# Block-sparse attention and a gated FFN in one kernel: a new start, recalibrated plan durations, and new load and work orders

## The chip, the cores and the metric

One core of one Trainium2 chip (trn2). The metric is the device time of one execution in microseconds (us). Kernels are compared in rounds on the same chip. Some executions come out slower, most of them with a lower mean TensorE clock (of the kernel before, for example, 260.20 us at 0.986 against 254.04 at 1.000); runs are marked fast or slow. In the views, PE is TensorE and PEld its weight loads, ACT is ScalarE, DVE is VectorE, POOL is GpSimd, and SP is SyncE, which here only issues transfers.

## The reference

Attention for 4 batches, 8 heads, 768 positions, head size 64, with a block mask (neighbours, first and last blocks, three random blocks per row), then a gated FFN on the 3072 x 512 result:

```python
scores = np.matmul(q, k.transpose(0, 1, 3, 2)) / np.sqrt(D)
scores = np.where(mask, scores, -1e9)          # mask: 24 x 24 blocks of 32
attn = exp(scores - max); attn = attn / (sum(attn) + 1e-9)
x = np.matmul(attn, v)                         # then (tokens, 512)
h = (x @ w1) * (x @ w2) @ w3                   # d_ff 1024
out = h @ w_out                                # float32
```

## The kernel before

The kernel describes its work as tasks with durations and dependences. A small list scheduler (`Plan.run`) orders them before anything is built; the chip then executes that order, engine by engine. A wrong duration cannot make a wrong result, but it can put a waiting instruction in front of others on an engine that works in order.

The work of one score tile: 4 matmuls (TensorE, here PE) into PSUM, one exp (ScalarE, ACT), half of a multiplication by the mask (VectorE, DVE), 8 value matmuls. There are 144 tiles, 36 per batch: 4 head pairs x 3 groups of 256 queries x 3 parts of the keys. The FFN of 512 tokens is 64 + 32 matmuls of 512 columns, six times; w3 and w_out are first multiplied together (64 more). q and k must be transposed: the first `trb` = 8 pairs (b, pr) on PE, the rest by a DMA transpose that SP issues:

```python
# (parts that the argument touches; cuts marked ...)
PRM = dict(bias=0.4, ..., btc=0.5, near=0.12, soon=0.06, kprio=2.0, ..., trb=8, units="tttt", nat=4, big=10)
...
    # if PE has nothing to do in the plan, it runs a "spare" matmul on zeros
    if pe > free["PE"] + 0.12 and rest > free["PE"] - 0.1:
        w = self.spare(mode)                     # planned at 0.11 us each
...
    elif t.kind == "xbar":                       # a DMA transpose
        busy = [row for a, z, row in lanes if a < t.start + 1.25 <= z]
        more = 4.0 * max(busy) / 4096 if busy else 0.0
        t.end = t.start + 1.25 + more            # time on SP
        t.seen = t.end + 2.6 + more              # landing
...
    nc.scalar.preload_act_table_set("natural_log_exp_and_others")
...
    for nm, dst, src, at in (("qn", q32, qv, 4.0), ("kn", k32, kv, 5.0)):   # first q and k, both from SP
        ld = add(f"first {nm}", {SP: 0.43}, lambda t, ...: nc.sync.dma_start(out=dst, in_=src[0][:, 0:2]), ...)
        LD[nm, 0, 0] = add(f"cast {nm}", both(0.81, 0.5), ...)              # one cast on ACT or DVE
...
            else:                                # pairs beyond trb
                m = add(f"re {b}{pr}{x}", {DVE: 0.37}, ... T("qs", ...) <- T("qn", ...).rearrange("p h c d -> p c h d"))
                t = add(f"xb {b}{pr}{x}", {SP: 1.25}, ... nc.sync.dma_start(out=qkt, in_=qs, transpose=True), kind="xbar")
```

All other loads of q, k, v and the weights are issued by GpSimd, in the order of a table `LOADS` ("a01" is q and k of pair (0,1), "v00" v of pair (0,0), "p20" all three of pair (2,0), "30" a part of w3, "10" and "20" parts of w1 and w2, "o0" of w_out).

The softmax here doesn't subtract the row's maximum and nothing guards it: scores larger than these inputs give would overflow.

## Time and profile before

| | before |
|---|---|
| median of the runs with the prediction | 254.35 us (254.33 to 254.66) |
| span of the profiled execution | 252.7 us |
| PE / ACT / DVE busy | 95% / 74% / 69% |
| first score, tile 12, tile 48, PE's end | 9.88, 30.30, 76.51, 248.83 us |

"Tile n" is the time at which the weight load of score tile n starts. These four times turn a busy timeline into progress; the prediction shows the lines of the profile and how to read them.

### The profile page before, as it was taken

The numbers are of one execution on the slowest core, as the hardware profiler recorded it, in microseconds if no ns is written. First come the engines' busy times: TensorE is split into PE (matmuls) and PEld (weight loads), VectorE is DVE, ScalarE is ACT, GpSimd is POOL, SyncE is SP. The second block draws the span as 40 slices with busy tenths as digits, with TensorE's granted clock in tenths as the row PEclk, the third lists the DMA queues.
The fourth block names the chain that finished last, engine by engine and source line by source line (L and its number), as shares of the span: only waits on it lengthen the run. The fifth ranks groups of instructions, "written<-read, shape, count | busy, mean of one in ns | idle before, by whom it ended". The sixth has DMA issues, their size and how long they took to land.

```text
span 252.7 us, 6330 instructions
## 1 busy us (share of the span) xinstructions
PE 240.6 (95%) x2647; PEld 130.5 (52%) x2689; DVE 174.9 (69%) x305; ACT 186.4 (74%) x231; POOL 44.9 (18%) x73
## 2 busy tenths in 40 slices
PE   7989999997999999999999999999999999999993
PEld 5554655664555455455455445555555554444441
DVE  5696698899699897988856776878777754312320
ACT  3685788897889898889888888788988862323321
POOL 8635455444421360000000000000000000000000
PEclk9999999999999999999999999999999999999998
DMA  7999999999997899994142020231201223022013
GB/s 174 171 205 207 208 210 194 164 199 167 177 173 99 104 144 194 184 242 86 34 110 101 4 42 3 61 108 44 42 4 21 65 89 79 0 83 83 4 42 125
DMA packets 45793, 28.08 MB, mean 111 GB/s; under 512 B 27332, under 2 KB 40644, under 8 KB 45764
## 3 DMA queue, kind: packets, MB, share of 16 engines
q0 software_dynamic: 15872, 14.29, 38.2%
q1 hardware_dynamic: 29892, 13.38, 25.4%
q8 instruction: 21, 0.34, 0.6%
q14 instruction: 8, 0.07, 0.1%
HBM read 29.36 MB, written 6.29 MB: 141 GB/s over the span
## 4 chain that ended last, share of the span: by engine, by line
PE 86%; DVE 4%; DMA 4%; ACT 3%; issue 2%; SPq 0%
PE f L622 33%; PE f L642 17%; PE s L528 14%; PE o L551 14%; PE f L603 5%; DMA x<-xn 4%; PE o L397 2%; DVE e L538 2%; ACT e L534 2%; PE f L474 1%; PE f L591 1%; DVE xn L561 1%; ACT qkt L293 0%; DVE w3t L293 0%; SPq L574 0%
## 5 line engine op out<-in xcount | busy, mean ns | idle before, releaser
L534 ACT ACTIVATE e<-s 128x1024 bf16<-128x1024 f32 x144 | 139.6, 1025 | 13.5 <-PE s L528 12.8
L622 PE MATMUL f<-x,w 128*128 128x512 bf16 x359 | 90.4, 379 | 2.8 <-issue 1.0
L538 DVE TENSOR_TENSOR e<-e,mask 128x2048 bf16<-128x2048 bf16 x72 | 87.4, 1218 | 7.4 <-ACT e L534 7.1
L551 PEld LDWEIGHTS <-e 128*128 128x128 bf16 x1152 | 44.1, 97 | 22.9 <-DVE xn L561 6.5
L633 DVE TENSOR_TENSOR big<-f,a 128x512 bf16<-128x512 f32 x48 | 33.1, 689 | 32.0 <-PE f L622 24.9
L551 PE MATMUL o<-v,e 128*128 128x65 bf16 x1152 | 50.6, 194 | 0.8 <-DVE xn L561 0.4
L622 PEld LDWEIGHTS <-w 128*128 128x128 bf16 x384 | 32.4, 98 | 35.3 <-issue 6.7
L642 PE MATMUL f<-wf,big 128*128 128x512 bf16 x183 | 46.2, 380 | 0.9 <-issue 0.6
L630 ACT CAST a<-f 128x512 bf16<-128x512 f32 x48 | 28.2, 588 | 24.6 <-PE f L622 24.6
L528 PE MATMUL s<-qkt 64*128 64x256 bf16 x576 | 45.2, 272 | 0.7 <-ACT e L534 0.7
L528 PEld LDWEIGHTS <-qkt 64*128 64x128 bf16 x576 | 22.2, 94 | 27.5 <-issue 24.1
L642 PEld LDWEIGHTS <-big 128*128 128x128 bf16 x192 | 16.1, 98 | 17.3 <-issue 3.2
L293 ACT COPY ob<-f 128x512 f32<-128x512 f32 x20 | 11.7, 587 | 14.1 <-PE f L642 14.1
L561 DVE TENSOR_TENSOR xn<-o,rec 128x256 bf16<-128x256 f32 x48 | 20.4, 424 | 1.7
L559 DVE RECIPROCAL rec<-o 128x4 f32<-128x4 f32 x48 | 8.6, 179 | 17.3 <-PE o L551 17.3
L603 PE MATMUL f<-wo,w3t 128*128 128x512 bf16 x56 | 15.8, 380 | 0.6 <-issue 0.3
L331 POOL DMA_DIRECT2D qn<-in_q_dram x15 | 10.9, 727 | 18.9 <-DVE qs L483 5.3
L331 POOL DMA_DIRECT2D kn<-in_k_dram x15 | 10.8, 719 | 14.1 <-DVE qs L483 6.2
L331 POOL DMA_DIRECT2D vn<-in_v_dram x16 | 11.4, 716 | 8.2 <-DVE v L496 5.8
L397 PE MATMUL o<-zero 128*128 128x256 bf16 (+1 forms) x45 | 7.8, 331 | 1.5 <-DVE zero L394 1.5
L293 DVE COPY qkt<-f 128x768 bf16<-128x768 bf16 x13 | 7.1, 552 | 2.0 <-PE f L474 1.9
L603 PEld LDWEIGHTS <-w3t 128*128 128x128 bf16 x64 | 4.9, 98 | 5.0 <-issue 0.6
(54 smaller groups left out, 87.1 us busy)
## 6 DMA issues: line engine op xcount, KB each, us to landing
out_dram<-ob SPq DMA_DIRECT2D x24, 256.0 KB, 2.0
vn<-in_v_dram POOLq DMA_DIRECT2D x16, 192.0 KB, 7.8
qn<-in_q_dram POOLq DMA_DIRECT2D x15, 192.0 KB, 8.1
kn<-in_k_dram POOLq DMA_DIRECT2D x15, 192.0 KB, 8.1
big<-in_moe_w_dram POOLq DMA_DIRECT2D x8, 256.0 KB, 8.9
w<-in_moe_w_dram POOLq DMA_DIRECT2D x8, 256.0 KB, 9.7
wo<-in_moe_w_out_dram POOLq DMA_DIRECT2D x2, 512.0 KB, 9.4
q<-in_q_dram SPq DMA_DIRECT2D x1, 384.0 KB, 3.2
```

What stands on the lines that cost most here:

```text
L293: (nc.scalar.copy if t.eng == ACT else nc.vector.tensor_copy)(out, in_)
L331: t = add(name, {POOL: 0.73}, lambda t: nc.gpsimd.dma_start(out=out_of(), in_=src), deps=deps, writes=writes, kind="load", prio=seq[0])
L528: nc.tensor.matmul(s[:, h, k2 * QT:(k2 + 1) * QT], lhsT=z[64 * h:64 * h + 64, 1, kc * 128:(kc + 1) * 128], rhs=z[64 * h:64 * h + 64, 0, t3 ...
L534: exps.append(add(f"E {m} {j}", {ACT: 0.97}, lambda t, sk=sk, ek=ek, j=j: nc.scalar.activation(T(*ek)[:, j], T(*sk), AF.Exp, scale=1.0 / 8 ...
L538: tm = add(f"K {m}", {DVE: 1.23}, lambda t, ek=ek, t3=t3, kp=kp: nc.vector.tensor_tensor(T(*ek), T(*ek), mask[:, t3, kp:kp + 2, :].unsquee ...
L551: nc.tensor.matmul(o[:, qt, h, :], lhsT=e[:, j, h, lo:lo + 128], rhs=w[:, h, kc, :], start=kc == 0 and qt == 0 and h == 0, stop=kc == C - ...
L561: tx = add(f"xn {rk}", {DVE: 0.42}, lambda t, rk=rk, ok=ok, xk=xk, pr=pr: nc.vector.tensor_tensor(T(*xk)[:, :, 128 * pr:128 * pr + 128].re ...
L603: nc.tensor.matmul(T(*key), lhsT=T("w3t", i)[:, j, :], rhs=wo_sb[:, j, :], start=j == 0, stop=j == NF - 1)
L622: nc.tensor.matmul(T(*key), lhsT=w[:, c, f * 128:(f + 1) * 128], rhs=T(*xk)[:, c, :], start=c == 0, stop=c == 3)
L630: ta = add(f"a {i}{f}", {ACT: 0.58}, lambda t, ak=ak, key=ends["w1"][0]: nc.scalar.copy(T(*ak), T(*key)), deps=[ends["w1"][1]], reads=[end ...
L633: nc.vector.tensor_tensor(T(*hk)[:, 512 * (f % 2):512 * (f % 2) + 512], T(*key), T(*ak), op=ALU.mult),
L642: nc.tensor.matmul(T(*key), lhsT=T(*hk[f // 2])[:, 512 * (f % 2) + n * 128:512 * (f % 2) + (n + 1) * 128], rhs=wf_sb[:, f, :], start=f == ...
```

## The change

The intent: q and k of the first pair sooner (k issued from ACT's queue ahead of the table load, casts in halves on two engines, written in a layout that needs half as many transposes); plan durations from measurements; loads in a new order (q and k of batch 0 first); and scheduling parameters that were searched anew, `trb=6` among them, so that pairs (1,2) and (1,3) move to the DMA transpose.

```diff
-SEEN = {"PE": 0.22, "ACT": 0.10, "DVE": 0.10, "POOL": 0.12, "SP": 0.05}
-SWITCH = 0.095
-LOADS = ("a01 v00 v01 o0 o1 30 a02 v02 31 32 a03 v03 33 34 35 36 37 "
-         "10 20 11 21 12 22 13 23 p10 p11 p12 p13 "
-         "p20 p21 p22 p23 p30 p31 p32 p33")
+SEEN = {"PE": 0.195, "ACT": 0.15, "DVE": 0.135, "POOL": 0.12, "SP": 0.05}
+SAME = {"PE": 0.0, "ACT": 0.13, "DVE": 0.118, "POOL": 0.05, "SP": 0.0}
+SWITCH = 0.1
+WARM = 4.9
+LOADS = ("a01 v00 a02 o1 a03 30 v01 v02 31 o0 32 34 33 v03 37 10 35 36 20 21 11 22 13 23 p13 12 "
+         "p10 p12 p11 p21 p20 p22 p23 p32 p30 p31 p33")
-PRM = dict(bias=0.4, ..., trb=8, units="tttt", ...)
+PRM = dict(bias=0.182, ..., trb=6, units='ttQt', ...)
@@ spares: planned at twice 0.11 us before WARM, so fewer of them
-                if pe > free["PE"] + 0.12 and rest > free["PE"] - 0.1:
+                if pe > free["PE"] + 0.12 * (2 if free["PE"] < WARM else 1) and rest > free["PE"] - 0.1:
+                    cost = w.costs["PE"] * (2 if free["PE"] < WARM else 1)
@@ start
-    nc.scalar.preload_act_table_set("natural_log_exp_and_others")
+    for nm, dst, src, eng, at in (("qn", q32, qv, SP, 3.9), ("kn", k32, kv, ACT, 4.3)):
+        ld = add(f"first {nm}", {eng: 0.46}, ... (nc.sync if t.eng == SP else nc.scalar).dma_start(...))
+        for hf in range(2):
+            LD[nm, 0, 0, hf] = add(f"cast {nm} {hf}", both(0.35, 0.22), ...)   # into [128, C, 2, D]
+    add("table", {ACT: 1.29}, lambda t: nc.scalar.preload_act_table_set(...), prio=-1.5)
-    t_zero = add("zero", {DVE: 0.2}, ...)
+    t_zero = add("zero", {POOL: 0.2}, ...)
@@ first pair: 6 full transposes each for q and k, copied out by halves (cut)
@@ all durations of the plan (cut), for example
-            exps.append(add(f"E {m} {j}", {ACT: 0.97}, ...
+            exps.append(add(f"E {m} {j}", {ACT: 0.915}, ...
```

## The prediction

> **What bounds the kernel now.** I read the page first: the busy shares, the slices, the chain that ended last.
>
> ```profile
> PE 240.6 (95%) x2647; PEld 130.5 (52%) x2689; DVE 174.9 (69%) x305; ACT 186.4 (74%) x231; POOL 44.9 (18%) x73
> ...
> PE   7989999997999999999999999999999999999993
> ...
> PEclk9999999999999999999999999999999999999998
> DMA  7999999999997899994142020231201223022013
> ...
> PE 86%; DVE 4%; DMA 4%; ACT 3%; issue 2%; SPq 0%
> ```
>
> PE (TensorE) is busy nearly everywhere and makes 86% of the chain, at full granted clock. But busy is not useful: in the first slices PE runs "spare" matmuls on zeros, and the DMA engines are full until about 100 us. So I split the run by the windows view (columns: stretch, its length, then busy us of PE, weight loads, DVE, ACT, POOL, clock, DMA share, GB/s).
>
> ```profile
> 6.80:69.00 62.20, 58.24 (x841) 35.33 (x850) 49.69 (x91) 49.95 (x61) 30.12 (x47) 1.00 1.28 192
> 69.00:206.90 137.90, 135.34 (x1579) 72.19 (x1602) 109.41 (x181) 119.71 (x144) 8.58 (x12) 1.00 0.51 89
> 206.90:248.90 42.00, 41.71 (x204) 19.10 (x206) 11.79 (x19) 14.10 (x25) 0.00 (x0) 1.00 0.16 54
> ```
>
> Then the timeline of the start, and the chain in order of time.
>
> ```profile
> 0.74 1.28 ACT L324 ACT_TABLE_LOAD   x1 [0.74 <-PEq L677]
> 1.25 0.46 SPq L347 DMA_DIRECT2D k<-in_k_dram  x1
> 1.47 5.41 PE L397 MATMUL o<-zero 128*128 128x256 bf16 x31 [1.47 <-DVE zero L394]
> 3.92 0.83 ACT L293 CAST qn<-q 128x768 bf16<-128x768 f32 x1 [1.91 <-DMA q<-in_q_dram]
> 5.15 0.16 DVE L418 CAST rand_f<-rand_sb 24x3 f32<-24x3 int32 x1 [1.27 <-DMA rand_sb<-in_sampled_blocks_dram]
> 6.03 0.54 DVE L293 CAST kn<-k 128x768 bf16<-128x768 f32 x1
> 6.81 0.53 PE L474 MATMUL f<-ident,qn 128*64 128x128 bf16 x12
> 8.23 0.53 PE L474 MATMUL f<-ident,kn 128*64 128x128 bf16 x12 [0.47 <-ACT qkt L293]
> 9.89 0.61 PE L528 MATMUL s<-qkt 64*128 64x256 bf16 x8
> ```
>
> ```profile
> 52.34 9.25 DMA x<-xn
> ...
> 67.43 1.30 PE f L622 x6
> 68.72 0.54 PE s L528 x8
> 69.27 0.97 PE f L622 x4
> 70.23 0.24 PE o L551 x8
> 70.48 0.86 PE f L622 x4
> ```
>
> q is cast by 4.75, but PE stays in its 31 spares until 6.81; k is cast only at 6.03, behind DVE work that waited for the random blocks. The first score is at 9.89, the first exp at 10.32. From about 69 us PE is simply full.
>
> **A ledger of PE work.** From the chain: a 512-column matmul takes 0.2165 us (32 of L642 in 6.91); four take 0.86, or 0.97 next to a score run, so a switch between 64-row scores and 128-row work costs 0.11 each way; eight score matmuls take 0.54 with one switch, so 0.0535 each; a value matmul 0.0304 (16 in 0.49); a transpose 0.0292 in pairs of half tiles (12 weight loads in 0.36), 0.0535 for w3; a mask matmul 0.107. The instruction order gives the counts: 576 score, 1152 value, 640 of 512 columns, 192 q/k and 64 w3 transposes, 20 mask, 76 score runs. Sum 215.6, plus 76 x 0.22 = 16.7: **232.3 us**. Check: by the ledger 171.6 us lie between score tile 48 and PE's end; the trace has that tile at 76.51 and the end at 248.86, 172.35. So after tile 48 only 0.75 us are wasted. Real work begins at 6.81, so 248.86 - 6.81 - 232.3 = 9.75 us of starvation lie almost wholly before tile 48. By tile: 0 at 9.88, 12 at 30.30 (ledger 17.8 by then), 42 at 68.78, 48 at 76.51. Thus **the end is tile 12's time, plus the ledger from there, plus the starvation still to come**; after PE, the last copy and store take 3.84 to the span's end, and the measured time is 254.35 - 252.7 = 1.65 over the span.
>
> **What the Trainium skill says.** (1) "TensorE: Matmul & The Clock Gate", Part 1: the array runs at half clock until some 3.4 us of sustained activity. The trace agrees: spares' weight loads are 0.213 us apart until 5.29 us, then 0.107; that is why 31 spares planned at 0.11 ran till 6.50 and held the transposes back. (2) "DMA: Bandwidth & Descriptors", Issuing engines are not separate DMA queues: transfers issued from several engines share the 16 DMA engines, and another issuer saves only sequencer time. The trace has k issued 0.51 us after q on one queue, landing 3.7 against 3.2 us after issue; so I grant the move of k some 0.5 us, not parallel bandwidth. (3) "ScalarE: Activation LUTs", What ACT_TABLE_LOAD costs: about 1283 ns; the trace has 1283 ns, from 0.74 to 2.02. Behind the k issue it ends near 2.5, before q lands at 3.9: no cost. (4) "TensorEngine Tiling (Array Packing)", Tiling Modes: changing the mode drains TensorE; the trace agrees with 0.11 us a switch.
>
> **The change part by part.**
> Start. k is issued near 0.74 and should land by 4.5. The casts are halved over ACT and DVE: about 0.3 instead of 0.83 (q, ACT) or 0.54 (k, DVE). Only 14 spares stand before the transposes; at 0.213 they end near 4.4. Casting into the [c,2,d] layout makes 12 full transposes of 24 half ones. The DVE order still has rand_f before k's half cast, and rand landed about 5.0; its issue moves up 0.5. So: q transposed 4.5 to 5.2, k cast by 5.2, transposed by 5.8, both copied by 6.6 (DVE's three random-block steps, 3 x 0.23, come between), first score near **6.7 instead of 9.88**. ACT now copies G (0.6 + 0.36) before the first exp, so that is near 7.4, not 10.3: 2.9 us won.
> First tiles. The loads now take q and k of all batch-0 pairs first (at the 0.2 MB/us of before, the third q/k pair lands near 10.5 and the fourth near 15.5), so scores no longer wait on w3 and w_out. Until tile 12 ACT paces it: 11 exps at 0.92 start to start (1.94 for two) and six copies of 0.59 make 13.7 us after 7.4: tile 12 at **21.1 instead of 30.3**. Of these 9.2 us most is only order: PE's ledger at tile 12 is 12.1, not 17.8, as w3 work has moved behind. Net 9.2 - 5.7 = 3.5 us.
> PE work. Two pairs (1,2) and (1,3) go from PE transposes to the DMA transpose: 48 fewer at 0.0292, 1.4 us. The first pair is neutral. Score runs rise from 76 to 78: +0.44. Ledger of after: **231.3**, so 1.0 us won. DVE exchanges PSUM copies of 0.56 for SBUF ones of 0.35; off the path.
> Rest of the schedule. New order, load order and a third batch by pair groups change no work, only starvation. Before, 248.86 - 30.30 - (232.3 - 17.8) = 4.1 us come after tile 12. The largest visible one is the first FFN matmul waiting for x: 9.25 us of transfer among full DMA engines. By its order, PE of after reaches the last value matmul of the second token group near 40.5 and the first FFN matmul after 12 us more work, which just covers such a transfer. I guess 2.3 us left: 1.8 won.
> Sum: 21.1 + (231.3 - 12.1) + 2.3 = 242.6 for PE's end; + 3.84 + 1.65 = **248.1 us**, 6.3 less than before.
>
> **Rivals.** (a) *The early start is hidden: loads set the pace.* For: DMA is full for 88 us, share over 1. Against: tile order shows it starved for order, not for total bytes, and after 69 us PE waits for no load. But if DVE (copies, masks and four e products in a row from 6.7) or a late v tile holds tile 12 near 23, and the four more DMA transposes at 40 to 60 us slow x and k, the time is 250 to 252: within 2%. (b) *Only the start counts* and the recalibrated order wins nothing: 3.5 + 1.0 = 4.5 us, about 249.9, within 2%. (c) *The new order removes nearly all starvation* (1 us left after tile 12, tile 12 at 20.5): 246.2. (d) ACT becomes the bound in the middle: it is at 119.7 of 137.9 us between 69 and 206.9, and its work there hardly changes; that costs at most 1 us.
>
> **Range and chances.** The firm part is 4.5 us; the rest rides on small waits that I can't see before it runs. The 2% line is 249.26 us, 1.2 above my number, and my error is about 2.3 us either way: 248.1, range 245.3 to 251.3; faster by over 2% 0.66, within 2% 0.33, slower 0.01.
>
> **What would show it.** Right: q's transposes before 5, first score 6.2 to 7.2, first exp before 8, tile 12 (the 49th score matmul) at 20 to 22.5, tile 48 at 69.5 to 72, then about 173 us to the end, with the chain from there all PE. Wrong: tile 48 later than 73 means that loads, DVE or the x transpose took the start back; more than 174.5 us from tile 48 to the end would mean a new wait in the full stretch, which I don't expect. A first score after 8 would mean that k or the random blocks land later than the single issue order suggests.

## The result

The changed kernel takes **265.69 us** (median of 4 runs, 262.20 to 268.15) against 254.50 (4 runs, 254.33 to 255.05). The ratio is 1.0358, 95% interval 1.0253 to 1.0462: slower. Ratios are the mean time of one kernel's fast runs over that of the other's of the same rounds, so they are not quite the ratio of the medians quoted. Only two of the four runs are marked fast (262.20 and 265.21), and the profiled one is slow (266.18). So what is read from it below is checked against e2, e3 and e16, whose profiles are fast ones.

The page of the changed kernel, the lines that answer to those of before:

```profile
PE 247.2 (94%) x2575; PEld 134.2 (51%) x2617; DVE 174.4 (66%) x307; ACT 186.6 (71%) x232; POOL 44.9 (17%) x74
...
PE   6999999999959958999999999999999999999994
...
PEclk9999999999988998999999999999999999999999
DMA  7999999999999999983632210232301224013013
...
PE 81%; DMA 11%; DVE 3%; ACT 2%; issue 2%; DVEq 0%
```

DMA has come onto the chain: 11% against 4%. PE has two holes, in the twelfth and the fifteenth slice, and the clock row has dips just after them. By stretch (columns as in the prediction):

```profile
5.50:76.60 71.10, 66.67 (x799) 39.46 (x809) 53.01 (x104) 53.24 (x68) 33.55 (x51) 1.00 1.28 179
76.60:106.90 30.30, 25.91 (x271) 13.79 (x278) 18.50 (x35) 19.96 (x23) 6.42 (x9) 0.89 1.42 150
106.90:217.00 110.10, 107.93 (x1296) 59.36 (x1319) 87.95 (x141) 96.34 (x114) 0.00 (x0) 1.00 0.32 69
```

From 107 us on PE is as full as before. The loss lies ahead of that, and the first stretch looks busy. The timeline of the start shows why busy is not progress there:

```profile
1.11 3.17 PE L400 MATMUL o<-zero 128*128 128x256 bf16 x14 [1.11 <-POOL zero L397]
5.02 0.51 ACT L295 CAST q0n<-q 128x384 bf16<-128x384 f32 x1 [2.49 <-DMA q<-in_q_dram]
5.58 0.82 PE L482 MATMUL f<-ident,q0n 128*128 128x128 bf16 x6 [1.31 <-DVE q0n L295]
8.86 0.85 PE L477 MATMUL f<-ident,qn 128*64 128x128 bf16 x12
23.78 1.50 PE L568 MATMUL o<-v,e 128*128 128x65 bf16 x24
```

The 14 spares end at 4.28, and then PE idles 1.3 us until q is cast. Twelve half transposes take 0.85 us; in the kernel before (the prediction's line at 6.81) they take 0.53. The 24 value matmuls at 23.78 take 1.50. PE runs at half clock: the trace's first clock record is the step to full rate, at **26.3 us** (before: 5.3 us). The clock row of the page shows 9 in these slices all the same, as it seems to show full rate where no record has been made yet.

The holes are in the chain in order of time:

```profile
66.19 10.41 DMA qkt<-qs
...
86.07 14.49 DMA qkt<-qs
```

Both are DMA transposes of q or k, from issue to landing.

**A table of progress.** I took the count of PE work from the prediction (instructions in their order times the durations there, spares left out, 0.11 us for a switch; the whole is 232.1 us before, with 75 runs of scores where the prediction counted 76, and 230.8 after) and subtracted it from the measured time of each tile. The difference is what PE has lost up to that tile, the first 5 to 7 us of waiting for data included:

| us lost by tile | 0 | 6 | 12 | 36 | 42 | 48 | 60 | 72 | end |
|---|---|---|---|---|---|---|---|---|---|
| before | 8.3 | 11.8 | 12.7 | 14.7 | 16.0 | 16.0 | 16.1 | 16.1 | 16.8 |
| after | 6.9 | 12.6 | 18.2 | 19.3 | 22.5 | 24.1 | 29.9 | 29.9 | 30.0 |

From tile 72 to the end neither row moves by more than 0.7: the count is good, and nearly all is decided by tile 60. The changed kernel loses 13.2 us more and has 1.3 us less work, 11.9 in all; the two profiled executions differ by 11.7. Two steps make it up: **tiles 0 to 12** (11.3 against 4.4) and **tiles 36 to 60** (10.6 against 1.4).

### The profile page after: what moved, and what is told of

Same layout as the page of the kernel before. It is cut to its first block, busy times and chain, and to the rows that moved or that the text cites.

```text
span 264.4 us, 6211 instructions
## 1 busy us (share of the span) xinstructions
PE 247.2 (94%) x2575; PEld 134.2 (51%) x2617; DVE 174.4 (66%) x307; ACT 186.6 (71%) x232; POOL 44.9 (17%) x74
## 4 chain that ended last, share of the span: by engine, by line
PE 81%; DMA 11%; DVE 3%; ACT 2%; issue 2%; DVEq 0%
PE f L639 28%; PE f L659 15%; PE s L545 14%; PE o L568 13%; DMA qkt<-qs 9%; PE f L620 5%; PE f L477 2%; PE f L450 2%; PE o L400 2%; DMA q<-in_q_dram 2%; ACT e L551 2%; PE f L608 1%; DVE e L555 1%; PE f L482 1%; DVE xn L578 0%
## 5 line engine op out<-in xcount | busy, mean ns | idle before, releaser
L639 PE MATMUL f<-x,w 128*128 128x512 bf16 x359 | 91.5, 383 | 1.8 <-issue 1.0
L568 PEld LDWEIGHTS <-e 128*128 128x128 bf16 x1152 | 45.8, 99 | 23.3 <-DVE e L555 6.0
L545 PE MATMUL s<-qkt 64*128 64x256 bf16 x576 | 48.9, 283 | 3.7 <-DMA qkt<-qs 2.8
L647 ACT CAST a<-f 128x512 bf16<-128x512 f32 x48 | 28.2, 589 | 18.9 <-PE f L639 18.9
L545 PEld LDWEIGHTS <-qkt 64*128 64x128 bf16 x576 | 23.1, 96 | 30.7 <-issue 22.4
L659 PEld LDWEIGHTS <-big 128*128 128x128 bf16 x192 | 16.3, 98 | 19.2 <-issue 3.1
L295 ACT COPY ob<-f 128x512 f32<-128x512 f32 x17 | 10.0, 587 | 16.1 <-PE f L659 15.0
L578 DVE TENSOR_TENSOR xn<-o,rec 128x256 bf16<-128x256 f32 x48 | 20.2, 421 | 1.0
L331 POOL DMA_DIRECT2D qn<-in_q_dram x15 | 10.9, 729 | 21.7 <-DVE qs L500 12.0
L331 POOL DMA_DIRECT2D vn<-in_v_dram x16 | 11.5, 719 | 9.9 <-DVE v L513 4.1
L331 POOL DMA_DIRECT2D kn<-in_k_dram x15 | 10.8, 720 | 13.2 <-DVE qs L500 6.8
L295 DVE COPY qkt<-f 128x768 bf16<-128x768 bf16 (+1 forms) x10 | 5.1, 514 | 4.5 <-PE f L477 4.3
## 6 DMA issues: line engine op xcount, KB each, us to landing
big<-in_moe_w_dram POOLq DMA_DIRECT2D x8, 256.0 KB, 10.3
```

What stands on the lines that cost most here:

```text
L295: (nc.scalar.copy if t.eng == ACT else nc.vector.tensor_copy)(out, in_)
L331: t = add(name, {POOL: 0.73}, lambda t: nc.gpsimd.dma_start(out=out_of(), in_=src), deps=deps, writes=writes, kind="load", prio=seq[0])
L545: nc.tensor.matmul(s[:, h, k2 * QT:(k2 + 1) * QT], lhsT=z[64 * h:64 * h + 64, 1, kc * 128:(kc + 1) * 128], rhs=z[64 * h:64 * h + 64, 0, t3 ...
L568: nc.tensor.matmul(o[:, qt, h, :], lhsT=e[:, j, h, lo:lo + 128], rhs=w[:, h, kc, :], start=kc == 0 and qt == 0 and h == 0, stop=kc == C - ...
L578: tx = add(f"xn {rk}", {DVE: 0.342}, lambda t, rk=rk, ok=ok, xk=xk, pr=pr: nc.vector.tensor_tensor(T(*xk)[:, :, 128 * pr:128 * pr + 128].r ...
L639: nc.tensor.matmul(T(*key), lhsT=w[:, c, f * 128:(f + 1) * 128], rhs=T(*xk)[:, c, :], start=c == 0, stop=c == 3)
```

## The experiments

The theory after the result: (1) 14 spares are too few to bring PE to full clock, which costs the first step; (2) the DMA transposes of q and k come too late, which costs the second. Rivals: the clock alone; the load order alone; the shorter durations; the new start itself. The table of progress for all runs stands at the end of this section.

### e1 and e16: ten more spares

```diff
+    spares = 0
     for t in log:
         t.go(t)
+        spares += t.name == "spare"
+        if t.name == "spare" and spares == 14:
+            for _ in range(10):
+                spare("N").go(t)
```

The plan and its order stay; only PE gets ten more matmuls on zeros.

> The changed kernel with ten more spare matmuls right after the first 14, nothing else, the planned order untouched. Theory (two causes: the PE clock stays at half rate until 26.3 us because 14 spares end at 4.3 us, and PE later waits for the DMA transposes of q and k): full rate from about 6 us, score tile 12 near 22 instead of 29.9 us, and the time falls by only part of that, 3 to 7 us, to 259 to 263, as the transposes still bind near 66 to 77 and 86 to 101 us. Rival A (the cold clock is all of it): 250 or less. Rival B (the early loads set the pace, the clock is a symptom): tile 12 stays at 28 or later and the time at 264 to 267.

Measured: 258.28 and 261.29 us (fast), 263.15 (slow), and one run of 1325.95, which the profile fell in. In that one every PE operation took some five times as long to the very end. It didn't happen again and I leave it out, unexplained. The ratio of the fast runs is 1.0172.

> e1 once more (the changed kernel with ten more spares, nothing else), for a profile of a normal execution. Theory: tile 12 near 22 us as in e3, the stall between tiles 36 and 60 still there (8 us or more lost), 258 to 263 us as in the three normal executions of e1.

Measured: 258.64 us (257.16 to 261.86), ratio 1.0135 (1.007 to 1.020), the profile fast. PE at the same places:

```profile
8.55 0.53 PE L477 MATMUL f<-ident,qn 128*64 128x128 bf16 x12
...
17.05 0.91 PE L568 MATMUL o<-v,e 128*128 128x65 bf16 x24
```

The same instructions in the same order take 0.53 and 0.91 us; the clock steps up at 6.5, tile 12 comes at 22.20 instead of 29.88, and 10.6 instead of 18.2 us are lost by then. So **the missing spares cost 7.6 us by tile 12**. In time, fast runs against fast runs, the ratio falls from 1.0358 to 1.0135, some 5.7 us; the cleaner pair e2 and e3 below, all of whose runs are fast and of the same rounds, gives 8 us. The second loss stays: 9.3 us from tile 36 to 60.

### e4: the kernel before with 14 spares

```diff
+    spares = 0
     for t in log:
+        spares += t.name == "spare"
+        if t.name == "spare" and 14 < spares <= 31:
+            continue
         t.go(t)
```

> The kernel before with only 14 of its 31 first spares, order otherwise untouched. Theory: PE stays at half clock far into the start, and the time rises by 3 to 8 us, to 257.5 to 262.5, with a wider spread. Rival (early loads set the pace, so a slow PE is hidden): 254 to 255.

Measured: 253.83 and 254.59 (fast), 257.97 and 262.82 (slow); the fast ones are at 0.9953 (0.9875 to 1.0032) of before. So this was half a miss: with 14 spares the kernel before is sometimes as fast as ever. The profile fell in the 262.82 run: the clock goes up at 4.9 us, down again at 8.3, and up again at 25.4 (with one more drop of 3.4 us at 114.1); tile 12 comes at 35.27 and 17.7 us are lost by then, 5 more than before. Here the transposes follow the 14 spares at once, and PE is busy for 3.35 of the 3.41 us before the step at 4.9; in the changed kernel the same 14 are followed by 1.3 us of idling. So the number of spares alone doesn't decide it; whether PE's work runs on without a gap may, though no run tests just that. I read the 31 spares as insurance: without them a run may warm in time or not. For the fast runs there is no profile that shows when they warmed. In the changed kernel none of four runs came near: the fastest, 262.20, is still 7.7 us over before.

### e2 and e3: trb back to 8

```diff
-... trb=6, units='ttQt', ...
+... trb=8, units='ttQt', ...        # e2; e3 = e2 and the ten spares of e1
```

> The changed kernel with trb=8 again: pairs (1,2) and (1,3) transposed on PE as before, the plan made anew. Theory: the start stays cold (tile 12 near 29 us), the waits of 10 and 14 us for the DMA transposes go, and what PE loses after tile 12 falls from 11.7 us to about 4: 256 to 260 us. Rival A (cold clock is all): 265 still. Rival B (it is the load order): 263 or more, with PE waiting for loads of q, k or v in their place.

Measured: 267.30 us (265.12 to 267.63), ratio 1.0440. A miss. As expected the start stays cold (tile 12 at 29.81, 18.2 lost, in a fast profile), but the wait has only moved, from pairs (1,2) and (1,3) to those of batch 2: 19.6 lost by tile 36, 29.5 by tile 60.

> Both edits together. Theory: the two costs add, 247 to 252 us, faster than the kernel before, with tile 12 near 22 us and about 4 us lost after it. If they overlap (a late start also hides transposes), 253 to 257.

Measured: 258.62 us (257.94 to 259.06), ratio 1.0124 (1.0072 to 1.0176). Also a miss, and an instructive one: up to tile 48 only 12.3 us are lost, 3.7 fewer than before, and tile 48 comes at 72.13, **at the late edge of where the prediction had it** (69.5 to 72). Then 8.7 us go between tiles 48 and 60, though the tiles of batch 2 start at 72. In that stretch DVE stands, in its order, at copies that re-lay q and k for batch 2 (2.80, 2.15 and 2.21 us), and the mask products behind them wait too. A line of the chain, and the second of these copies:

```profile
72.90 13.98 DMA qkt<-qs
```

```profile
86.97 0.36 DVE L500 COPY qs<-kn 128x768 bf16<-128x768 bf16 x1 [2.15 <-DMA qkt<-qs]
```

A copy needs a buffer that an earlier transpose must first have read. The profile puts the wait of 2.80 us, which ends at 83.33, down to a load of v, but the transpose issued at 68.97 lands at 83.24, just before it.

### e5 to e8: one part of the new schedule undone at a time

```diff
 e5: before.py + the new start (loads, casts, layout, table, WARM) + ten spares
 e6: e1 with the LOADS of before
 e7: e1 with the PRM of before
 e8: e1 with SEEN, SAME and all durations of before
```

> The kernel before (its load order, parameters and durations) with the new start alone, and ten more spares so that PE gets warm. Theory (the start itself is sound, the new schedule is what costs): first score near 7.9 instead of 9.9, none of the long waits for transposes between 65 and 105 us, 251 to 254 us. Rival (the halved casts and the second issuing queue are themselves bad): 256 or more.

Measured: 255.50 us (255.25 to 257.00), ratio 1.0015. The first score comes at 7.59 instead of 9.88, yet tile 12 at 31.25 against 30.30: with the old load order the k of the third and fourth pair, which lands after its q, is there only at 20.4 and 26.0 us in e5 (19.9 and 25.3 in before, 11.5 and 16.0 in after), and an earlier start just waits for them longer. No long wait for a transpose appears. So the rival's number came nearer, but not for its reason: the new start isn't bad, it is worth nothing alone.

> The changed kernel with ten more spares and the load order of before. With e7 and e8 it undoes one of three parts of the new schedule. If the load order causes the late waits (loads of batches 2 and 3 and the DMA transposes meeting on the same engines): 252 to 256 us, the waits gone. If it doesn't: 258 to 263, as e1.

Measured: 261.62 us, ratio 1.0231.

> The changed kernel with ten more spares and all scheduling parameters of before (trb=8, units tttt, the biases and priorities). If the parameters (more pairs by DMA transpose, third batch by pair groups) cause the late waits: 250 to 255 us. If not: 257 to 262, as e3, which had only trb=8.

Measured: 260.90 us, ratio 1.0216.

> The changed kernel with ten more spares and the durations and delays of before in the plan (new load order, new parameters). If the shorter durations make a plan that is too tight, with transposes issued into full DMA engines and DVE standing behind them: 252 to 256 us. If not: 258 to 263, as e1.

Measured: 261.81 us, ratio 1.0256. None of the three restores the time (all three ratios are above the 1.0135 of e16, in other rounds); each has its own long wait for transposes (6 to 14 us lost between tiles 36 and 60). So no single part of the table is the culprit. What they share, and e5 doesn't, is that the first transposes of q and k are issued at 51 to 63 us; in before they start at 70, in e5 at 84. The hour alone can't be it, though: in e2 they start at 69.7, and it stalls. What goes with the stall is how much is loaded just then. The queue of GpSimd's loads between 70 and 90 us (packets, MB, share of the 16 DMA engines), in before and in e2:

```profile
q0 software_dynamic: 1924, 1.39, 63.2%
```

```profile
q0 software_dynamic: 3205, 2.32, 93.7%
```

In e4 and e5, which don't stall in that stretch either, it moves 1.51 and 1.26 MB; in after, e16 and e3, which do, 2.24, 2.48 and 2.65. This is a comparison of traces; what it suggests, e13 tests.

### e9 to e11: the buffers, the plan's number, no transposes

```diff
 e9:  "qs": 4 -> 8 buffers          (all three from e3)
 e10: more = 4.0 * max(busy) / 4096 -> 8.0 * max(busy) / 4096
 e11: trb=8 -> trb=16
```

> The kernel of e3 (258.6 us; warm, trb=8) with 8 instead of 4 buffers for the re-laid q and k that the DMA transposes read. Theory: between tile 42 and tile 60 e3 takes 31.5 us where its PE work needs about 23, because DVE, which works in order, stands at re-layout copies until a transpose frees a buffer, and each transpose takes SP 4 to 5 us while loads fill the DMA engines. If the buffers are the tie: tile 42 to 60 in 23 to 26 us, 251 to 255 us. If the transposes themselves come too late for PE: 256 to 259.

Measured: 259.05 us, ratio 1.0183; 21.1 lost by tile 60, as e3. With more buffers DVE only runs into the next wait: at these copies it stands 7.7 us for transposes in all, against 5.3 in e3.

> The kernel of e3 with the plan told that a DMA transpose takes 3.0 instead of 1.5 us longer while q, k, v loads run (factor 8 for 4). Theory: the plan then sets the re-layout copies and their users later, so DVE stands less: 253 to 257 us. Rival (the transposes are simply too slow beside the loads, wherever they stand in the order): 258 to 260.

Measured: 257.56 us (256.49 to 258.89), ratio 1.0132. Tile 60 comes at 88.60 instead of 95.83 and the total loss falls from 21.1 to 19.0, so a truer number for the transpose moves the stall in the profiled execution. The time is 0.6 above the upper end of what was expected, and the ratio is no better than the 1.0124 of e3, so a gain in time isn't shown.

> The kernel of e3 with all pairs transposed on PE (trb=16), so no DMA transposes of q and k at all. PE work rises by 192 x 0.029 = 5.6 us. Theory: the stretch from tile 42 to 60 then has no wait for a transpose of q or k, tile 60 comes at 88 to 91 us instead of 95.8, and the time is 253 to 257: about even with e3 or a little under. Rival (the loads of batches 2 and 3 are what PE waits for, not the transposes): tile 60 still at 94 or later and 261 to 266 us.

Measured: 267.26 us, ratio 1.0503. Half a hit: tile 60 comes at 86.36, so the stall is indeed one of transposes, but the time is far off. The work is 5.9 us more, and another 6.9 us are lost between tiles 60 and 78: attention runs ahead of the FFN (232 FFN matmuls by tile 138, against 324 in e3), and PE has short waits, for exps and for DVE's products among others. I haven't broken this second loss down.

### e12: the first k from SP again

```diff
-    for nm, dst, src, eng, at in (("qn", q32, qv, SP, 3.9), ("kn", k32, kv, ACT, 4.3)):
+    for nm, dst, src, eng, at in (("qn", q32, qv, SP, 3.9), ("kn", k32, kv, SP, 4.3)):
```

> The kernel of e3 with the first k issued from SP behind q, as before, one look. In e3 q lands 4.3 us after issue against 3.2 in the kernel before. Theory (two transfers at once share the DMA engines, so the second queue delays q and hardly brings k earlier): q lands near 4.0 to 4.3 and k near 5.2, first score within 0.4 us of 7.89. Rival (the second queue helps): first score at 8.5 or later.

259.70 us. The timelines of the start, e3 first, then e12:

```profile
5.11 0.51 ACT L295 CAST q0n<-q 128x384 bf16<-128x384 f32 x1 [2.58 <-DMA q<-in_q_dram]
5.53 0.51 ACT L295 CAST k0n<-k 128x384 bf16<-128x384 f32 x1
7.89 0.33 PEld L545 LDWEIGHTS <-qkt 64*128 64x128 bf16 x8 [0.87 <-DVE qkt L295]
```

```profile
4.08 0.51 ACT L295 CAST q0n<-q 128x384 bf16<-128x384 f32 x1 [2.06 <-DMA q<-in_q_dram]
5.07 0.51 ACT L295 CAST k0n<-k 128x384 bf16<-128x384 f32 x1 [0.48 <-DMA k<-in_k_dram]
7.52 0.45 PEld L545 LDWEIGHTS <-qkt 64*128 64x128 bf16 x8 [0.58 <-DVE qkt L295]
```

With two issuers at once q is there 1.03 us later. k is no earlier: the changed kernel's page has it 4.5 us from issue (0.74) to landing, so at 5.2, and in e12 its cast starts at 5.07. The other traces agree: q lands at 4.9 to 5.2 in fourteen profiles with k on ACT (that of e1 left aside), and at 3.8 to 4.1 in the five with k on SP (before, e4, e12, e17, e18). The first score comes 0.37 us later in e3 than in e12, but that much is not shown to be the queue's: with the new casts it stands at 7.3 to 8.2 in the profiles with k on ACT, and at 7.52, 7.75 and 7.88 in e12, e17 and e18. The second queue delays q and wins nothing that these traces show.

### e13: without the loads of batches 2 and 3

```diff
-        t = add(name, {POOL: 0.73}, lambda t: nc.gpsimd.dma_start(out=out_of(), in_=src),
+        t = add(name, {POOL: 0.73}, lambda t: nc.gpsimd.memset(out_of(), 0.01) if name.startswith("ld") and writes[0][1] >= 2
+                else nc.gpsimd.dma_start(out=out_of(), in_=src),
```

This is e3 with memsets for those loads: a wrong result, the same order on every engine.

> The kernel of e3 with the loads of q, k, v of batches 2 and 3 replaced by memsets on GpSimd; wrong result on purpose, the order on every engine the same. Theory (transposes are slow because these loads fill the DMA engines): a transpose keeps SP for 1.2 to 2 us instead of 4 to 5 between 65 and 95 us, tile 48 to 60 takes 15.5 to 18 us instead of 23.7, no second drop of the clock, and the time falls to 249 to 252 us. Rival (the transposes are late by their own order or dependences): tile 48 to 60 still over 22 us and 257 to 259 us.

Measured: 251.83 us (250.74 to 252.22), ratio 0.9880 (0.9834 to 0.9927), against 1.0124 for e3. The transposes of q and k in the views of their source lines (minimum, median, maximum time on SP in ns), in before, after, e3 and e13:

```profile
L486 SPq DMA_TRANSPOSE qkt<-qs x16: 1211/1288/2838, 70.2 to 119.5; - x16
```

```profile
L503 SPq DMA_TRANSPOSE qkt<-qs x20: 1212/1396/5686, 55.7 to 133.0; - x20
```

```profile
L503 SPq DMA_TRANSPOSE qkt<-qs x16: 1209/1302/5039, 61.8 to 123.5; - x16
```

```profile
L504 SPq DMA_TRANSPOSE qkt<-qs x16: 1209/1237/2098, 63.2 to 116.0; - x16
```

Between 60 and 105 us such a transpose keeps SP for 3.20 us on average in after, 3.03 in e3, 1.76 in before and 1.31 in e13; after 105 us, when the loads are all but over, 1.2 to 1.5 on average in all of them. From tile 48 to 60 e13 loses nothing (13.6 and 13.6; e3 12.3 and 21.0), and the clock stays up until the end:

```profile
PEclk9999999999999999999999999999999999999998
```

So **the loads of q, k, v that run at the same time make the transposes slow**. Besides those loads, only the values in the tiles and 24 memsets on GpSimd differed. One rival remains in e13 alone: a memset is also ready sooner than a load, so PE and DVE no longer wait for late data either. Against it stand the transposes' own times above, and e11, where all loads are there and the transposes are not: it loses 3.1 us from tile 48 to 60, against 8.7 in e3.

### e14, e15, e17, e18: towards a better version

```diff
 e14: e3, LOADS from the 25th on as in before: "... 13 23 12 p10 p11 p12 p13 p20 p21 ... p33"
 e15: e14 and the 8.0 of e10
 e17: e15, trb=10, first k from SP
 e18: e15, trb=12, first k from SP
```

> The kernel of e3 with the new load order for the first 24 loads and the order of before from there on (w1 chunk 2 first, then pairs in their order of use). If the order of the later loads matters: q and k of the pairs that PE needs come earlier, tile 42 to 60 in 24 to 28 us instead of 31.5, 252 to 256 us. If not: 258 to 260.

Measured: 256.52 us (256.37 to 256.79), ratio 1.0069. Below what was expected of "not", just above the other; 6.3 us are still lost from tile 48 to 60. The interval (1.0022 to 1.0117) overlaps that of e3, so the gain is likely and not settled.

> e14 with the plan's longer DMA transposes of e10 (257.6 us). If both help and add: 250 to 254 us, faster than or even with the kernel before. If only one matters: as the better of e10 and e14.

Measured: 255.61 us, ratio 0.9996 (0.9909 to 1.0084), with a spread of 252.62 to 257.08. Even with the kernel before, not better.

> e15 (255.6 us, spread 252.6 to 257.1) with the pairs (2,0) and (2,1) transposed on PE (trb=10: 48 x 0.029 = 1.4 us more PE work) and the first k issued from SP. Theory: the transposes that remain start later, when fewer loads run; some of e15's 6.9 us lost between tiles 42 and 66 comes back: 251 to 255 us. Rival (PE transposes of batch 2 only move the wait): 255 to 258.

Measured: 259.47 us, ratio 1.0163. A miss: 13.6 lost by tile 60, then 6.5 at once, while DVE stands 5.0 us at one copy for a transpose of the remaining pairs.

> The same with all four pairs of batch 2 on PE (trb=12, 2.8 us more PE work): 251 to 256 us if the stall goes wholly; over 257 if, as in e11, PE comes to wait for exps with the FFN work not yet ready.

Measured: 256.11 us (255.26 to 256.52), ratio 1.0064, just above the range. The stall is gone (14.7 lost by tile 60, 14.8 at the end, the least of all right results), but PE has 3.6 us more work than before, and that eats it. Its eight transposes start at 87.1 us, when the loads are nearly over, and keep SP 1.24 us on average.

No version beats the kernel before by a margin that the runs settle.

### The table of progress for all

| us lost by tile | 0 | 12 | 36 | 48 | 60 | 72 | end | PE work | ratio |
|---|---|---|---|---|---|---|---|---|---|
| before | 8.3 | 12.7 | 14.7 | 16.0 | 16.1 | 16.1 | 16.8 | 232.1 | 1 |
| after (slow profile) | 6.9 | 18.2 | 19.3 | 24.1 | 29.9 | 29.9 | 30.0 | 230.8 | 1.036 |
| e16 after, warm | 7.0 | 10.6 | 12.4 | 20.9 | 21.7 | 21.7 | 21.7 | 230.8 | 1.014 |
| e2 trb 8, cold | 6.9 | 18.2 | 19.6 | 20.2 | 29.5 | 29.5 | 29.6 | 232.2 | 1.044 |
| e3 trb 8, warm | 6.9 | 10.5 | 11.8 | 12.3 | 21.0 | 21.0 | 21.1 | 232.2 | 1.012 |
| e4 before, 14 spares (slow profile) | 7.2 | 17.7 | 19.7 | 19.9 | 20.0 | 23.5 | 25.0 | 232.1 | 0.995 |
| e5 start only | 6.7 | 13.7 | 14.9 | 17.3 | 17.3 | 17.3 | 17.4 | 232.4 | 1.002 |
| e6 old loads | 7.0 | 13.7 | 19.4 | 25.4 | 25.6 | 25.5 | 25.6 | 230.8 | 1.023 |
| e7 old parameters | 6.6 | 10.6 | 13.2 | 13.6 | 22.5 | 22.6 | 23.4 | 232.2 | 1.022 |
| e8 old durations | 6.5 | 11.4 | 12.2 | 21.5 | 25.8 | 25.8 | 25.8 | 231.3 | 1.026 |
| e9 8 buffers | 7.2 | 10.8 | 12.2 | 12.6 | 21.1 | 21.1 | 21.2 | 232.2 | 1.018 |
| e10 slower transposes in the plan | 6.8 | 10.3 | 11.7 | 16.6 | 16.6 | 19.0 | 19.0 | 232.0 | 1.013 |
| e11 no transposes by DMA | 7.2 | 11.2 | 12.6 | 14.0 | 17.1 | 22.8 | 24.3 | 238.1 | 1.050 |
| e12 k from SP (one look) | 6.6 | 10.8 | 12.3 | 12.7 | 21.5 | 21.5 | 21.6 | 232.4 | none |
| e13 without loads 2, 3 (wrong result) | 6.8 | 10.4 | 13.0 | 13.6 | 13.6 | 13.6 | 13.6 | 232.2 | 0.988 |
| e14 old tail of loads | 6.8 | 10.3 | 11.8 | 12.2 | 18.5 | 18.9 | 18.7 | 232.2 | 1.007 |
| e15 e14 and e10 (slow profile) | 7.1 | 10.6 | 12.1 | 16.2 | 16.2 | 19.2 | 19.2 | 232.2 | 1.000 |
| e17 trb 10 (slow profile) | 6.8 | 10.5 | 12.1 | 13.6 | 13.6 | 20.4 | 20.5 | 234.3 | 1.016 |
| e18 trb 12 | 6.9 | 10.6 | 12.2 | 13.7 | 14.7 | 14.7 | 14.8 | 235.7 | 1.006 |

The losses are those of the profiled execution, the ratios those of the fast timed runs; e1, whose profile is the run of 1326 us, is left out.

**The clock, again.** A stall costs more than its length. In e3 (the windows view of PE alone: stretch, length, busy us, clock, DMA share, GB/s):

```profile
82.58:85.99 3.41, 1.11 (x12) 1.00 1.06 157
85.99:89.40 3.41, 1.87 (x15) 0.51 1.40 185
```

After a window in which PE was busy for 1.11 of 3.41 us its clock halves, and it stays halved for 6.8 us (to 92.9). In after there are two such drops of 3.4 us, at 77.5 and 98.0, right behind the two waits. Two times 3.4 us at half rate make a mean clock of 0.987, the value of both of its slow runs; in the fast run of 262.20 it is 1.000. So for the changed kernel the slow mark may be no accident of the chip but a part of the mechanism. That is a reading: only one slow run has a trace, and no fast run of this kernel has one. The mean clock doesn't count the cold start, which has no record.

## Why the prediction was wrong

By its own steps:

- **"Only 14 spares stand before the transposes; at 0.213 they end near 4.4."** The time is right (4.28), the sign is wrong. It was booked as a gain of some 2 us in the start of the transposes. Fourteen spares at 0.213 are 3.0 us of activity, less than the 3.4 that the same prediction quoted from the page on the clock gate just before, and q, which landed at 5.0 instead of 3.9, left PE idle for 1.3 us behind them; the fact was used to explain the kernel before and not asked of the kernel after. The clock stayed at half rate until 26.3 us, which cost 7.6 us by tile 12 (after against e16). This is the first failed step. That ten more spares do away with it is shown; why the clock then stayed down so long, with PE busy for over 99% of every 3.4 us from 5.9 to 22.9, is not.
- **"I grant the move of k some 0.5 us."** It won nothing that the traces show: k landed at 5.27 instead of the 4.5 it assumed (4.92 before), and q at 4.99 instead of 3.9 (4.05 with k behind it on SP, e12). The first score came at 7.89 instead of 6.7; e3 and e16, warm, have it at 7.89 and 8.01 too, so the clock isn't the reason. The halved casts were mis-sized as well: about 0.3 us was assumed, and a half took 0.51 on ACT and 0.53 to 0.56 on DVE, where the whole cast of k had taken 0.54 on DVE before. So halving won no time on DVE; whether the new layout is the reason was not tested.
- **Tile 12 at 21.1.** With a warm PE it is at 22.1 (e3) and 22.2 (e16). The step held but for the clock.
- **PE work 231.3, 1.0 less than before.** 230.8 and 1.3 by the same durations; right, with 75 and 76 runs of scores where the prediction had 76 and 78. (A reading of no consequence: the warm spares are 0.109 us apart by the trace, not 0.107.) Between tile 72 and the end the loss moves by no more than 0.8 us in any kernel but e4 and e11 (1.5 each), which bears out the count.
- **"I guess 2.3 us left"** after tile 12: it was 11.8 in after, 11.1 in e16, 10.6 in e3. This is the second failed step. The least was 3.2, in e13, without the loads; e5 and e18 had 3.7 and 4.2. The prediction asked which transfer the FFN waits for, and not what an earlier attention front does to the transposes: it brings them into a fuller load stream (in after 2.24 MB instead of 1.39 from 70 to 90 us), where they keep SP for 3.20 us on average instead of 1.76, DVE stands at their re-layout copies, and PE's clock drops behind the stall. Rival (a) named "the four more DMA transposes at 40 to 60 us" and sized them at no more than 2 to 4 us in all; and e3 shows that the four weren't even needed for the stall.
- **"DVE exchanges PSUM copies of 0.56 for SBUF ones of 0.35; off the path."** The copies are shorter, but each is a place at which DVE can wait for a DMA. Off the path in busy time, on it in order (2.15 us at the one copy shown for e3).

The sum: tile 12 was 8.8 us late (29.88 - 21.1) and 9.5 us more were lost after it (11.8 - 2.3), 18.3 in all, less 0.1 each for the work after tile 12 and for what follows PE; the measured 266.18 of that execution is 18.1 over 248.1. The signs that the prediction named for being wrong came: tile 48 at 85.53, later than 73, and 175.25 us from there to PE's end, over 174.5. Of the 2.9 us that the start promised some 2 were there at tile 12 in the warm runs (10.5 lost in e3, 12.7 in before) and of no use: e5 shows that they need the new load order, and e3 that the new load order needs faster transposes.

What stays open: when the fast runs of e4 got warm with 14 spares, why a clock that is down stays down for some 20 us of busy PE, which part of the new schedule fills the hour of the transposes with loads (undone one at a time, none brings the time back), and the run of 1326 us of e1. It is also not shown which property of the loads slows the transposes (their small packets, their number, or the shared engines as such), only that taking them away does away with it.

## What to carry to other kernels

When a change removes filler work from TensorE, ask what that work was for: check that the activity left runs on without a gap into the first real work, and look at the duration of equal instructions, not at the clock row, to see whether it did. When a front of work is brought forward, list the transfers that come forward with it and see what is in the DMA engines at that hour; a transpose measured in an empty stretch (here 1.2 us) says little about one among loads (here 3 on average, up to 5.7). And count work against time by milestones (here the tiles): it separates in one table what the busy shares hide, and it shows where a plan's win is given back.

## What the Trainium skill lacked or had wrong

- "TensorE: Matmul & The Clock Gate", Part 1, states a warm-up of some 3.4 us of sustained activity. 31 spares in before agree, with the step at 5.3 us, and so does the missing step after the 14 spares and 1.3 us of idling in after. Its table of the two states has the clock fall back after an idle window; here it fell after windows that were far from idle: PE was busy 1.11 of 3.41 us in e3, and 2.36 of 3.41 in e4 (window 4.88 to 8.29, busy time as the profile models it). And a PE that the profile shows busy nearly all the time at half clock stayed there for 17 us in e4 (8.3 to 25.4) and from 5.6 to 26.3 in after, which sustained activity alone doesn't explain.
- The same page, on reading the clock: nothing says that a profile may show full clock before the first recorded step. In after the page's clock row is 9 up to 26.3 us while twelve half transposes take 0.85 us instead of 0.53.
- "DMA: Bandwidth & Descriptors", Issuing engines are not separate DMA queues, says that a second issuer saves only sequencer time; this agrees (k no earlier), but it lacks the price: the cast of the first transfer started 1.03 us later (5.11 in e3 against 4.08 in e12).
- "DMA: Bandwidth & Descriptors", DMA Transpose (X-bar), has no figure for transposes beside loads: here 1.2 us on the issuing engine when the loads are over, up to 5.7 us, and up to 15 us to landing, among GpSimd's loads (after), and 2.1 us at most with the loads of batches 2 and 3 taken away (e13).
